# Grid search proved by counts with a branch into the exact search, batch rows turned by VectorE, and aligned load buffers, in an attention and expert-routing kernel

## The chip, the cores and the metric

The kernel runs on one core of one Trainium2 chip. The core has five engines, each with an instruction stream of its own: TensorE (PE; its weight loads are shown as PEld), VectorE (DVE), ScalarE (ACT), GpSimd (POOL) and SyncE (SP, which here only issues transfers). They wait for each other by semaphores. The metric is the time of one execution on the device, in microseconds; lower is better.

## The reference

Attention over 8 batches, 12 heads, 448 tokens and 64 features per head, with a sigmoid instead of a softmax, and behind it a mixture of 8 experts in which each expert takes exactly 448 of the 3584 tokens:

```
scores = scale * np.matmul(q, k.transpose(0, 1, 3, 2)) - np.log(S)
attn = 1.0 / (1.0 + np.exp(-scores))
attn_out = np.matmul(attn, v)
x = attn_out.transpose(0, 2, 1, 3).reshape(B * S, H * D)
logits = x @ w_gate
for idx in np.argsort(-logits.flatten()):
    tok, e = (int(idx) // E, int(idx) % E)
    if assigned[tok] >= 0 or counts[e] >= cap:
        continue
    assigned[tok] = e
    counts[e] += 1
for e in range(E):
    mask = assigned == e
    out[mask] = np.maximum(x[mask] @ w1[e], 0.0) @ w2[e]
```

All data are float32. `cap` is 448. Tokens of one batch have nearly equal logits, because the sigmoids are all near 1/449 and a head's output is near the mean of V.

## The kernel before, in words

**Attention.** A loop goes over 48 pairs of heads (`pairs`, six for each batch). For a pair, VectorE transposes K and Q into `kqT` (`turn`, L408) from load buffers `nkq` that SP and GpSimd fill two groups ahead (`load`). ScalarE rounds them (`kqH`, L416), VectorE takes the rest (`kqL`, L417), so that a product of float32 is three products (L433). ScalarE makes the sigmoids (`at`, L423). One pair later TensorE multiplies with V (`av`, L457 and L463), and VectorE copies the outcome into `xt` (L465, L467), with features on partitions. A list `bg` of small jobs is worked off, one a pair: `logits` (L478, added into `LE`, L480) and `rows` (L489 to L496). `rows` transposes half a chunk of 112 tokens on TensorE, copies it to `xr` and stores it in `xs`, a table in DRAM with a row for each token. With `LATE = 7` only the first batch is turned so during attention (copied by VectorE); the rows of the other seven wait in `late`.

**Routing.** `Router.phase(k)` is a generator that settles one expert after the other: take away what is settled (`remove`), build keys so that each token counts for its best expert alone (`keys`, L151 to L158), find in each expert's list the 448th largest key (`search`), take the expert with the largest one (`pick`), and make its list of tokens (`place`, `lists`, ending with `r_idx`, L298). `search` fixes the bits of the threshold in 16 steps of two bits. Each step counts the keys over three thresholds (three L178, with the count read out) and adds the counts of 16 rows: by a product on TensorE (L190) for `k == 0`, by two 32-wide transposes and a reduction on VectorE (L194 to L200) for later experts. The first phase runs by itself, with the late rows between its steps (`LATE_PER_STEP`). The later phases run between the matmuls of the experts.

**Experts.** `moe(kx)` yields after every matmul with a planned cost, which runs a clock; when the clock says so, the next piece of the routing is recorded (`T_KEYS` ... `T_BT` are the planned waits behind each piece) or one of the `chores`: the gather of the next expert's rows (`gather`, L625), their transposes into `xh` and `xl` (`xturn`, L639 to L643), and the turning back of the output. `prepare` puts gathers and transposes on that list as soon as the next expert's list is recorded, and `flush` issues at the end of an expert what is still due. Weights are streamed: `load_w` reads the chosen expert's number into a register of SP (L585) and issues one transfer for each unit (L592, L596), ScalarE rounds (`wh`, L603), GpSimd or, for the first two units, VectorE takes the rest (`wl`, L605). Everything is recorded in program order, and each engine works in that order.

Of the kernel before, what the change touches and what calls it, by code (L numbers as in the profile page):

```python
# [7 lines left out]
F32 = mybir.dt.float32  # L8
# [14 lines left out]
LATE = 7  # L23
XT_BUFS = 7
XA_BUFS = 5
AT_BUFS = 8
YT_BUFS = 3
LATE_PER_STEP = 3
LATE_KEYS = 7
T_KEYS, T_KE, T_STEP, T_DVE, T_KAP, T_PICK, T_TOT, T_OH, T_BT = 3600, 2100, 2050, 2025, 500, 2600, 600, 3800, 600  # L30
# [6 lines left out]
Y_DVE, Y_WAIT = 6, 4000  # L37

# [10 lines left out]
def route_consts(nc, cp, K):  # L49
# [66 lines left out]
    K.gfin = _s32(g)  # L116


class Router:
# [4 lines left out]
    def __init__(self, tc, K, st, wk, psum):  # L124
        self.tc, self.nc, self.K = tc, tc.nc, K
        self.wk, self.ps = wk, psum
        self.ei = None
        self.ML = st.tile([112, 2, 8, 16], F32, name="ML")
        self.csum = st.tile([1, 1], F32, name="csum")
        tc.nc.vector.memset(self.csum, -28.0)  # L130

# [30 lines left out]
    def search(self, pe):  # L162

        nc, K, wk, KT = self.nc, self.K, self.wk, self.KT
        p = self.bank()
        for g in range(2):
            nc.tensor.transpose(p[:, g * 112:(g + 1) * 112],
                                KT[:, g].rearrange("p e c -> p (e c)"), K.ident[:112, :112])
        KE = wk.tile([128, 224], F32, name="r_KE")
        nc.vector.tensor_copy(KE, p[:, :224])  # L170
        T, JP = K.c0, None
        X = None if pe else self.bank().bitcast(I32)
        for st in range(16):
            sh = 30 - 2 * st
            cnt = wk.tile([128, 3], BF, name="r_cnt") if pe else K.CN
            for i in range(3):
                junk = wk.tile([128, 224], BF, name="r_junk")
                nc.vector.tensor_scalar(junk, KE, T[:, i:i + 1].bitcast(F32), None, OP.is_ge, OP.add,  # L178
                                        accum_out=cnt[:, i:i + 1])
            nX = None  # L180
            if 0 < st < 15:
                nX = wk.tile([128, 3], I32, name="r_X") if pe else X[:, 4 * (st % 2):4 * (st % 2) + 3]
            acc = wk.tile([128, 1], F32, name="r_acc")
            j2 = wk.tile([128, 3], F32, name="r_j2")
            if pe:
                if nX is not None:
                    nc.vector.tensor_scalar(nX, K.kk[:, st + 1], JP, None, OP.bitwise_xor)
# [4 lines left out]
            else:  # L192
                ct = wk.tile([128, 32], F32, name="r_ct")
                nc.vector.transpose(ct, cnt)  # L194
                if nX is not None:
                    nc.vector.tensor_scalar(nX, K.kk[:, st + 1], JP, None, OP.bitwise_xor)
                s2 = wk.tile([128, 2], F32, name="r_s2")
                nc.vector.tensor_reduce(s2, ct.rearrange("p (e r) -> p e r", r=16), AX.X, OP.add)
                ct2 = wk.tile([128, 32], F32, name="r_ct")
                nc.vector.transpose(ct2.rearrange("p (e r) -> p e r", r=16), s2[:, :, None].to_broadcast([128, 2, 16]))  # L200
                tot = ct2[:, :3]
            nc.vector.tensor_scalar(j2, tot, 447.5, TWO23, OP.is_ge, OP.add, accum_out=acc)
            nJ = wk.tile([128, 1], I32, name="r_J")
            if st == 0:
                J = wk.tile([128, 1], I32, name="r_J0")
                nc.vector.tensor_scalar(J, acc.bitcast(I32), sh, None, OP.logical_shift_left)
                PF = wk.tile([128, 1], I32, name="r_PF")
                nc.vector.tensor_scalar(PF, J, 31, -1, OP.arith_shift_right, OP.bitwise_xor)
                nc.vector.tensor_scalar(nJ, PF, _s32(0x80000000), J, OP.bitwise_or, OP.bitwise_xor)
                T = wk.tile([128, 3], I32, name="r_T")  # L210
                nc.vector.tensor_scalar(T, K.kk[:, 1], nJ, None, OP.bitwise_xor)
            else:
                if st < 15:
                    T = wk.tile([128, 3], I32, name="r_T")
                    nc.vector.scalar_tensor_tensor(T, acc.bitcast(I32).to_broadcast([128, 3]), sh, nX,
                                                   OP.logical_shift_left, OP.bitwise_xor)
                nc.vector.tensor_scalar(nJ, acc.bitcast(I32), sh, JP, OP.logical_shift_left, OP.bitwise_xor)
            JP = nJ
            if not pe:
                yield T_DVE  # L220
        kap = wk.tile([128, 1], I32, name="r_kap")
        nc.vector.tensor_scalar(kap, JP, K.gfin, None, OP.bitwise_xor)
        self.kap = kap.bitcast(F32)

    def pick(self):
# [3 lines left out]
        nc.tensor.transpose(p[:112, :128], self.kap.to_broadcast([128, 112]), K.ident)  # L229
        kr = p[:112, :128].rearrange("p (e c) -> p e c", c=16)[:, :, 0]  # L230
        km = wk.tile([112, 1], F32, name="r_km")
        nc.vector.tensor_reduce(km, kr, AX.X, OP.max)
        w = self.w8 = wk.tile([112, 8], F32, name="r_w8")
# [14 lines left out]
        self.ei = wk.tile([1, 1], I32, name="r_ei", bufs=4)  # L248
# [22 lines left out]
    def lists(self):  # L271
# [25 lines left out]
        idx = wk.tile([128, 4], I32, name="r_idx", bufs=4)  # L297
# [14 lines left out]
    def left(self):  # L312
# [8 lines left out]
        self.ei = wk.tile([1, 1], I32, name="r_ei", bufs=4)  # L321
        nc.vector.tensor_copy(self.ei, self.csum)

    def phase(self, k):
        if k:
            self.remove()
        if k < 7:
            self.keys()
            yield T_KEYS
            yield from self.search(k == 0)  # L330
            yield T_KAP
            self.pick()
# [7 lines left out]
def moe_attention(tc, q, k, v, w_gate, w1, w2, out):  # L340
# [7 lines left out]
    with contextlib.ExitStack() as ctx:  # L348
# [7 lines left out]
        ps_s = pctx.enter_context(tc.tile_pool(name="pa_s", bufs=3, space=PSUM))  # L356
        ld = actx.enter_context(tc.tile_pool(name="ld", bufs=2))
# [123 lines left out]

        XR = {}

        def rows(b, c, hf, eng):
            if hf == 0:
                XR[b] = xa.tile([CP, DM], F32, name="xr", bufs=XA_BUFS)
            p = ps_t.tile([128, 512], F32, name="tp")
            for i in range(3):
                nc.tensor.transpose(p[:CP, i * 128:(i + 1) * 128], XT[b][:, hf * 3 + i, c * CP:(c + 1) * CP], ident)  # L489
            dst = XR[b][:, hf * 384:(hf + 1) * 384]  # L490
# [396 lines left out]
```

## Time and profile before

| | us |
|---|---|
| median of three runs | 882.42 (881.5 to 882.93) |
| profiled execution, whole | 883.43 |
| its span, first to last instruction | 881.7 |
| attention, TensorE's first product to its last of V | 7.5 to 278 |
| logits, first routing, late rows | 278 to 332.8 |
| experts | 332.8 to 861.7 |
| last half of the output | 861.7 to 881.7 |

Times in views count from the start of the span. A line with L and a number is that line of the kernel. A group's row names the line, the engine, the operation, what is written and read, the shape, the count, then the busy time in us and the mean of one in ns, and behind the last bar the idle time ahead of it with what ended it. In a timeline, the first number is the start and the second the length.

### The profile page before, as it was taken

Reading aid. Unit: us, or ns where it says so; the run is one execution under the profiler, and the core shown is the slowest. Engines: PE = TensorE matmul, PEld = TensorE weight load, DVE = VectorE, ACT = ScalarE, POOL = GpSimd, SP = SyncE. Lnnn points to the kernel's source line nnn. Section 1 sums busy time; section 2 is a strip of 40 time slices with the busy share of each in tenths; the row PEclk is TensorE's granted clock in tenths of the full one; section 3 lists DMA queues with packets and bytes.
Section 4 is the critical chain, followed back from the end, with each engine's and each line's share of the span. In section 5 each row is a group of like instructions: output and inputs, shape, how many; then the busy total and the mean of one; then the engine's idle time right before and its main releaser. Section 6 shows DMA issues by size and latency. Waiting matters only on the chain.

```text
span 881.7 us, 16211 instructions
## 1 busy us (share of the span) xinstructions
PE 840.1 (95%) x5467; PEld 636.9 (72%) x5467; DVE 542.4 (62%) x2060; ACT 447.3 (51%) x612; POOL 466.0 (53%) x446
## 2 busy tenths in 40 slices
PE   6999999999999739998999999999999999999996
PEld 3455555555554528987988988988888888999996
DVE  4566555555554988958859879779779631332130
ACT  6777677777775734434434434534434344541420
POOL 9744344444410014854864873873883883851561
PEclk9999999999999979998999999999999999999999
DMA  9866766666621855443442442551542542634643
GB/s 173 165 142 149 153 126 127 127 126 127 126 43 54 270 192 154 120 138 123 128 136 97 160 155 81 177 162 57 189 153 72 170 153 90 209 96 141 203 151 126
DMA packets 213811, 122.16 MB, mean 139 GB/s; under 512 B 153344, under 2 KB 202496, under 8 KB 213728
## 3 DMA queue, kind: packets, MB, share of 16 engines
q1 hardware_dynamic: 200992, 87.62, 38.2%
q0 software_dynamic: 10880, 33.28, 12.0%
q8 instruction: 43, 0.70, 0.3%
q10 hardware_dynamic: 1856, 0.23, 0.2%
q14 instruction: 40, 0.33, 0.1%
HBM read 96.76 MB, written 24.31 MB: 137 GB/s over the span
## 4 chain that ended last, share of the span: by engine, by line
PE 82%; DVE 11%; issue 2%; DMA 2%; POOL 1%; SPq 1%; ACT 1%; POOLq 0%; DVEq 0%; ACTq 0%
PE tp L457 13%; PE sc L433 11%; PE sc L736 9%; PE sc L734 9%; PE sc L738 9%; PE sc L773 6%; PE sc L775 6%; PE sc L771 6%; DVE r_junk L178 4%; PE tp L463 2%; PE sc L443 2%; PE tp L639 2%; PE tp L652 2%; PE tp L478 1%; PE rt L289 1%
## 5 line engine op out<-in xcount | busy, mean ns | idle before, releaser
L605 POOL TENSOR_TENSOR wl<-wr,wh 128x768 fp32r<-128x768 f32 (+1 forms) x96 | 204.9, 2145 | 124.5 <-ACT wh L603 116.8
L423 ACT ACTIVATE at<-sc,bias 128x896 f32<-128x896 f32 x168 | 161.5, 1006 | 67.1 <-PE sc L443 38.4
L383 POOL DMA_DIRECT2D nkq<-in_q_dram x188 | 118.4, 646 | 116.2 <-DVE kqT L408 104.6
L775 PE MATMUL sc<-hh,wl 128*128 128x448 f32 (+2 forms) x400 | 150.2, 375 | 0.0
L738 PE MATMUL sc<-xh,wl 128*128 128x448 f32 (+2 forms) x396 | 146.2, 369 | 0.0
L736 PE MATMUL sc<-xl,wh 128*128 128x448 f32 (+2 forms) x396 | 146.0, 369 | 0.1
L773 PE MATMUL sc<-hl,wh 128*128 128x448 f32 (+2 forms) x400 | 145.5, 364 | 0.2 <-POOL hl L746 0.2
L734 PE MATMUL sc<-xh,wh 128*128 128x448 f32 (+2 forms) x396 | 145.0, 366 | 0.0
L771 PE MATMUL sc<-hh,wh 128*128 128x448 f32 (+2 forms) x400 | 144.1, 360 | 0.4 <-issue 0.4
L178 DVE TENSOR_SCALAR_CACHE_REDUCE r_junk<-r_KE,r_T 128x224 bf16<-128x224 f32 x315 | 123.2, 441 | 0.1
L603 ACT ACTIVATE wh<-wr 128x768 fp32r<-128x768 f32 (+1 forms) x112 | 102.0, 939 | 36.3 <-DMA wr<-in_moe_w_dram 23.4
L457 PE MATMUL tp<-at,nv 128*64 128x448 f32 x576 | 118.8, 548 | 0.0
L746 POOL TENSOR_TENSOR hl<-yt,hh 128x896 fp32r<-128x896 f32 x32 | 68.4, 2136 | 48.8 <-ACT yt L745 47.2
L742 ACT ACTIVATE hh<-sc 128x896 fp32r<-128x896 f32 x32 | 29.5, 921 | 117.1 <-PE sc L738 117.1
L417 DVE TENSOR_TENSOR kqL<-kqT,kqH 128x896 fp32r<-128x896 f32 (+1 forms) x49 | 52.5, 1073 | 58.5 <-ACT kqH L416 58.4
L773 PEld LDWEIGHTS sc<-hl,wh 128*128 128x128 f32 x400 | 75.8, 189 | 6.8 <-issue 1.1
L625 POOL DMA_INDIRECT xr<-xs,r_idx x32 | 32.0, 999 | 91.2 <-ACT wh L603 80.2
L736 PEld LDWEIGHTS sc<-xl,wh 128*128 128x128 f32 x396 | 75.2, 190 | 6.7 <-issue 0.5
L457 PEld LDWEIGHTS tp<-at,nv 128*64 128x64 f32 x576 | 37.1, 136 | 59.1 <-issue 56.6
L734 PEld LDWEIGHTS sc<-xh,wh 128*128 128x128 f32 x396 | 75.2, 190 | 6.0
L771 PEld LDWEIGHTS sc<-hh,wh 128*128 128x128 f32 x400 | 76.0, 190 | 4.8 <-issue 0.6
L738 PEld LDWEIGHTS sc<-xh,wl 128*128 128x128 f32 x396 | 75.1, 190 | 5.3
(166 smaller groups left out, 1266.1 us busy)
## 6 DMA issues: line engine op xcount, KB each, us to landing
wr<-in_moe_w_dram SPq DMA_DIRECT2D x64, 384.0 KB, 3.0
wr<-in_moe_w_dram SPq DMA_DIRECT2D x48, 512.0 KB, 3.6
nkq<-in_k_dram SPq DMA_DIRECT2D x192, 56.0 KB, 2.6
xs<-xr SPq DMA_DIRECT2D x32, 336.0 KB, 3.3
nkq<-in_q_dram POOLq DMA_DIRECT2D x188, 56.0 KB, 2.7
nv<-in_v_dram SPq DMA_DIRECT2D x92, 96.0 KB, 2.7
ys<-yt SPq DMA_DIRECT2D x20, 112.0 KB, 1.9
nr<-in_v_dram SPq DMA_DIRECT2D x46, 32.0 KB, 2.2
```

The costliest lines, as they stand in the source:

```text
L178: nc.vector.tensor_scalar(junk, KE, T[:, i:i + 1].bitcast(F32), None, OP.is_ge, OP.add, accum_out=cnt[:, i:i + 1])
L383: qn.dma_start(t[o:o + 32, n], rws[x])
L423: nc.scalar.activation(a, p[:, :, :S], AF.Sigmoid, bias=bias, scale=1 / math.sqrt(D))
L457: nc.tensor.matmul(p[j * 64:j * 64 + 64, :S], nat["v", b, g][:, h0 + j, c, :], AT[b, pr, c][:, j, :], start=(c == 0), stop=(c == 2 and pr ...
L603: nc.scalar.activation(hi, raw[u], AF.Copy)
L605: eng.tensor_tensor(lo, raw[u], hi.bitcast(F32), OP.subtract)
L734: nc.tensor.matmul(ph[:, f, lo:hi], wh[:, a, fs], xh[:, dd, lo:hi], start=st, stop=False)
L736: nc.tensor.matmul(ph[:, f, lo:hi], wh[:, a, fs], xl[:, dd, lo:hi], start=False, stop=False)
L738: nc.tensor.matmul(ph[:, f, lo:hi], wl[:, a, fs], xh[:, dd, lo:hi], start=False, stop=en)
L771: nc.tensor.matmul(py[:, d2, :w], wh[:, a, dsl], h1, start=st, stop=False)
L773: nc.tensor.matmul(py[:, d2, :w], wh[:, a, dsl], h2, start=False, stop=False)
L775: nc.tensor.matmul(py[:, d2, :w], wl[:, a, dsl], h1, start=False, stop=(j == 1 and a == 3))
```

## The change

Several edits go together.

**The search.** `scale`, new, takes from the logits of the first four batches the power of two `D` at or under the largest, and makes a grid from it: steps of `D`, `D/4`, `D/16` and so on. `search` now refines the edge by two bits a step on that grid, in floating point: 4 steps from `-2D` for the first expert, and 9 steps from the former threshold less `D` for the others. It ends with the lower edge `base` of an interval, and one more count of the keys at that edge. `pick` transposes the edges and sums the counts on TensorE, and adds the counts of the experts that have the largest edge. If that sum is exactly 448, the edge parts the same tokens as the 448th key does. The sum is read into a register of VectorE and compared; otherwise a branch leads into `exact`, the former 16 steps wholly on VectorE.

```diff
+        self.tc.mark_branch_hint_location(f"found{k}", "LikelyTaken", [mybir.EngineType.DVE])
+        self.base = base
+        self.cnt = wk.tile([128, 1], BF, name="r_cn1")
+        self.count(base, self.cnt)
...
-        nc.tensor.transpose(p[:112, :128], self.kap.to_broadcast([128, 112]), K.ident)
-        kr = p[:112, :128].rearrange("p (e c) -> p e c", c=16)[:, :, 0]
-        km = wk.tile([112, 1], F32, name="r_km")
+        nc.tensor.transpose(p[:, :128], self.base.to_broadcast([128, 128]), K.ident)
+        nc.tensor.matmul(p[:, 128:256], self.cnt.to_broadcast([128, 128]), K.G, start=True, stop=True)
+        tr, cr = (p[:, o:o + 128].rearrange("p (e c) -> p e c", c=16)[:, :, 0] for o in (0, 128))
+        few, kr = wk.tile([128, 8], F32, name="r_few"), wk.tile([128, 8], F32, name="r_kr")
+        nc.vector.tensor_scalar(few, cr, 447.5, NONE, OP.is_lt, OP.mult)
+        nc.vector.tensor_tensor(kr, tr, few, OP.subtract)
+        km = self.km = wk.tile([128, 1], F32, name="r_km")
         nc.vector.tensor_reduce(km, kr, AX.X, OP.max)
+        nc.vector.tensor_tensor(few, cr, few, OP.add)
+        nc.vector.scalar_tensor_tensor(few, kr, km, few, OP.is_equal, OP.mult)
+        ok = wk.tile([128, 1], F32, name="r_ok")
+        nc.vector.tensor_reduce(ok, few, AX.X, OP.add)
+        found = nc.vector.value_load(ok[:1].bitcast(I32))
+        with self.tc.If(found != FOUND, preferred_fallthrough_block=True, label=f"found{k}"):
+            self.exact(kr)
+            nc.vector.tensor_reduce(km, kr, AX.X, OP.max)
```

`N_FIRST, N_FAST = 4, 9`; `FOUND` is 448.0 as an integer. `scale` runs in `bg` after the fourth batch:

```diff
+            nc.vector.tensor_scalar(a.bitcast(I32), LE[:, 0].bitcast(I32), 0x7FFFFFFF, None, OP.bitwise_and)
+            nc.vector.tensor_reduce(m[:, :1], a, AX.X, OP.max)
+            nc.tensor.transpose(p[:, :128], m[:, :1].to_broadcast([128, 128]), ident)
+            nc.vector.tensor_reduce(m[:, 1:], p[:, :128], AX.X, OP.max)
...
+    for r in range(N_FAST + 1):
+        nc.vector.tensor_scalar(K.cw[:, r], t8, 4.0 ** -r, None, OP.mult)
```

VectorE's order in the first routing, at the end of the search, before. `r_J` holds the bits found, `r_kap` the threshold, `r_km` the largest one, `r_w` the marks of the experts that have it:

```order
L178 TENSOR_SCALAR r_junk,r_cnt<-r_KE,r_T 128x224 x3
L202 TENSOR_SCALAR r_j_3968,r_acc<-rt 128x3
L217 TENSOR_SCALAR r_J<-r_acc,r_J 128x1
L222 TENSOR_SCALAR r_kap<-r_J 128x1
L232 TENSOR_REDUCE r_km<-rt 112x1
L234 SCALAR_TENSOR_TENSOR r_w_3998<-rt,r_km,c_rank 112x8
```

And now, after 4 steps in place of 16, up to the branch:

```order
L239 TENSOR_SCALAR r_base<-r_acc,c_kw,r_base 128x1
L184 TENSOR_SCALAR r_junk,r_cn_3553<-r_KE,r_base 128x224
L292 TENSOR_SCALAR r_few<-rt 128x8
L293 TENSOR_TENSOR r_kr<-rt,r_few 128x8
L295 TENSOR_REDUCE r_km<-r_kr 128x1
L296 TENSOR_TENSOR r_few<-rt,r_few 128x8
L297 SCALAR_TENSOR_TENSOR r_few<-r_kr,r_km,r_few 128x8
L299 TENSOR_REDUCE r_ok<-r_few 128x1
L300 TENSOR_LOAD r_ok
L301 COMPARE_AND_BRANCH
```

Behind the branch stand the 165 instructions of `exact` with their closing jump, then a short block that only evens the semaphore and jumps, and then L306, the former L234. The four other engines have a plain jump at each of the seven places.

**The rows.** `LATE` goes from 7 to 1. `turn_rows`, new, transposes two pairs of heads of a batch on VectorE in blocks of 32 by 32 during attention, and stores them when four or two pairs are together (eight transfers a batch on SP). Only the last batch's rows are still turned by TensorE (`late_rows`, six transposes and two copies by ScalarE for each chunk of 112).

```diff
+            if old and old[1] % 2 and old[0] < B - LATE:
+                bg.append(lambda b=old[0], pr=old[1]: turn_rows(b, pr))
...
+            nc.vector.transpose(XR[b].rearrange("p i r j -> p r i j")[:, pr - 1 - h:pr + 1 - h],
+                                XT[b][:, pr - 1:pr + 1].rearrange("p r (i t) -> p r i t", t=32))
+            if pr == h + n - 1:
+                for a in range(4):
+                    o, w = 128 * h + 32 * n * a, 32 * n
+                    nc.sync.dma_start(xs[b * S:(b + 1) * S, o:o + w].rearrange("(i t) c -> t i c", t=32),
+                                      XR[b][32 * a:32 * a + 32].rearrange("t i r j -> t i (r j)"))
```

TensorE's order between the last batch's logits and the search, before (`rt` is the router's tile in PSUM, `LE` the logits, `r_KT` the keys):

```order
L478 MATMUL tp<-xt,wgz 32x112 x8
L489 MATMUL tp<-ident,xt 112x128 x3
L139 MATMUL rt<-ident,LE 112x128 x2
L489 MATMUL tp<-ident,xt 112x128 x21
L167 MATMUL rt<-ident,r_KT 128x112 x2
L489 MATMUL tp<-ident,xt 112x128 x9
L190 LDWEIGHTS c_G
L190 MATMUL rt<-r_cnt,c_G 128x3
L489 MATMUL tp<-ident,xt 112x128 x9
```

And now:

```order
L552 MATMUL tp<-xt,wgz 32x112 x8
L583 MATMUL sc<-ident,xt 112x128 x6
L149 MATMUL rt<-ident,LE 112x128 x2
L583 MATMUL sc<-ident,xt 112x128 x18
L177 MATMUL rt<-ident,r_KT 128x112 x2
L229 LDWEIGHTS c_G
L229 MATMUL rt<-r_cnt,c_G 128x3
```

Six row transposes instead of three stand ahead of the logits' own, 18 instead of 21 ahead of the keys', and none between the steps.

**The order of features.** Rows turned in blocks of 32 stand in `xs` in another order of features, so the rows of `w1` are read in that order. A unit of the first layer then takes three transfers (`j == 0`) or five (`j == 1`) instead of one, of the same bytes:

```diff
-                src = w1[ds(gate[kx], 1)].rearrange("e (a p) f -> p (e a) f", p=128)
-                nc.sync.dma_start(t, src[:, 3 * j:3 * j + 3, i * 256:(i + 1) * 256])
+                src = w1[ds(gate[kx], 1)].rearrange("e (r a j) f -> a (e r) j f", a=4, j=32)[:, :, :, i * 256:i * 256 + 256]
+                for a in range(3 * j, min(3 * j + 3, 4)):
+                    nc.sync.dma_start(t[:, a % 3], src[a, :4])
+                for a in range(4 * j):
+                    nc.sync.dma_start(t[64 * (a % 2):64 * (a % 2) + 64, 1 + a // 2], src[a, 4:])
```

**Planned times and buffers.** The planned waits of the routing are new (`T_DVE` 2025 to 2290, `T_KAP` 500 to 3000, `T_PICK` 2600 to 5200). For experts after the first, gathers are due 25 us of the clock into the expert and the row transposes 9 us later, 2.3 us apart (after the first gathers: 5 us later and 1.7 us apart):

```diff
-                t0 = clock[0]
-                lag = max(5000, min(14000, start + 40000 - t0))
+                t0 = max(clock[0], start + X_AT) if kx else clock[0]
+                lag = 9000 if kx else 5000
...
-                        chores.append((t0 + lag + 1500 * j, kx + 1,
+                        chores.append((t0 + lag + (X_GAP if kx else 1700) * (2 * j + hf), kx + 1,
```

`r_ei` and `r_idx` have 8 buffers instead of 4, `xt` 3 instead of 7. A pad of 192 bytes a partition moves the load buffers; `nkq` and `nv` now begin at multiples of 512 bytes.

More of the change, by code (lines that the diff above doesn't have):

```diff
@@ L160, in keys, with ends @@
         self.KT = KT
-    def search(self, pe):
-        nc, K, wk, KT = self.nc, self.K, self.wk, self.KT
+    def ends(self):
+        nc, KT = self.nc, self.KT
         p = self.bank()
@@ L167, in search @@
             nc.tensor.transpose(p[:, g * 112:(g + 1) * 112],
[L168 to L174, printed above, removed]
+                                KT[:, g].rearrange("p e c -> p (e c)"), self.K.ident[:112, :112])
+        self.KE = self.wk.tile([128, 224], F32, name="r_KE")
@@ new lines, in ends, with count, sums @@
+        nc.vector.tensor_copy(self.KE, p[:, :224])
+    def count(self, T, cnt):
+        junk = self.wk.tile([128, 224], BF, name="r_junk")
+        self.nc.vector.tensor_scalar(junk, self.KE, T, None, OP.is_ge, OP.add, accum_out=cnt)
+    def sums(self, cnt, ct, s2, ct2, between=None):
+        nc = self.nc
+        nc.vector.transpose(ct, cnt)
+        if between:
+            between()
+        nc.vector.tensor_reduce(s2, ct.rearrange("p (e r) -> p e r", r=16), AX.X, OP.add)
+        nc.vector.transpose(ct2.rearrange("p (e r) -> p e r", r=16), s2[:, :, None].to_broadcast([128, 2, 16]))
+        return ct2[:, :3]
@@ new lines, in search @@
+    def search(self, k):
+        nc, K, wk = self.nc, self.K, self.wk
+        pe = k == 0
+        rows = range(N_FIRST) if pe else range(1, N_FAST + 1)
+        if pe:
+            T, base = K.T0, K.base0
+        else:
+            base = wk.tile([128, 1], F32, name="r_base")
+            nc.vector.tensor_scalar(base, self.km, K.D, None, OP.subtract)
+            T = wk.tile([128, 3], F32, name="r_T")
+            nc.vector.tensor_scalar(T, K.kw[:, 1], base, None, OP.add)
+        X = None if pe else self.bank()
+        for r in rows:
@@ L183, in search, with ahead @@
+            def ahead(r=r, nX=nX, base=base):
+                if nX is not None:
+                    nc.vector.tensor_scalar(nX, K.kw[:, r + 1], base, None, OP.add)
             acc = wk.tile([128, 1], F32, name="r_acc")
@@ L185, in search @@
             if pe:
-                if nX is not None:
-                    nc.vector.tensor_scalar(nX, K.kk[:, st + 1], JP, None, OP.bitwise_xor)
+                ahead()
                 yield T_STEP
@@ L329, in phase @@
             yield T_KEYS
-            yield from self.search(k == 0)
+            self.ends()
+            yield from self.search(k)
             yield T_KAP
-            self.pick()
+            self.pick(k)
         else:
@@ new lines, in moe_attention, with late_rows @@
+        XR = {}
+        def late_rows(b, c):
+            x = xa.tile([CP, DM], F32, name="xr", bufs=XA_BUFS)
+            p = ps_s.tile([128, 2, 512], F32, name="sc")
+            for r in range(NP):
+                o = r % 4 * 128
+                nc.tensor.transpose(p[:CP, r // 4, o:o + 128], XT[b][:, r, c * CP:(c + 1) * CP], ident)
+            for h, n in ((0, 4), (1, 2)):
+                nc.scalar.copy(x[:, 512 * h:512 * h + 128 * n].rearrange("p (a r j) -> p r a j", r=n, j=32),
+                               p[:CP, h, :128 * n].rearrange("p (r a j) -> p r a j", r=n, j=32))
+            nc.sync.dma_start(xs[b * S + c * CP:b * S + (c + 1) * CP], x)
@@ L531, in moe_attention @@
                     bg.append(lambda b=b: logits(b, range(NP)))
[L532 to L537 removed]
+                if b == 3:
+                    bg.append(scale)
+                for c in range(NCH if b >= B - LATE else 0):
+                    late.append(lambda b=b, c=c: late_rows(b, c))
         for f in bg:
```

130 lines of the change are left out of this document (75 added, 55 removed).

## The prediction

> **What bounds the kernel now.** I read the page's first part (busy time by engine) and the chain that ended last, then the busy time by stage. Columns of the second view: stretch, length, then busy time of TensorE, its weight loads, VectorE, ScalarE and GpSimd, the granted TensorE clock, the DMA engines' busy share and GB/s.
>
> ```profile
> PE 840.1 (95%) x5467; PEld 636.9 (72%) x5467; DVE 542.4 (62%) x2060; ACT 447.3 (51%) x612; POOL 466.0 (53%) x446
> PE 82%; DVE 11%; issue 2%; DMA 2%; POOL 1%; SPq 1%; ACT 1%; POOLq 0%; DVEq 0%; ACTq 0%
> ```
>
> ```profile
> 7.50:278.00 270.50, 270.39 (x2216) 137.87 (x2216) 150.62 (x208) 197.24 (x216) 121.64 (x204) 1.00 0.61 125
> ...
> 285.10:315.50 30.40, 23.19 (x155) 14.86 (x154) 27.52 (x176) 21.95 (x48) 0.00 (x0) 1.00 0.84 272
> 315.50:332.80 17.30, 5.32 (x53) 4.25 (x53) 13.21 (x37) 3.17 (x5) 4.13 (x6) 0.61 0.54 165
> 332.80:861.70 528.90, 523.05 (x2896) 464.42 (x2895) 342.69 (x1626) 215.65 (x325) 329.48 (x213) 0.99 0.44 137
> ```
>
> Attention (to 278) and the experts (332.8 to 861.7) are TensorE without a hole worth naming; only work taken from TensorE itself shortens them. The 54.8 us between belong to a chain on VectorE: TensorE's 23.19 us during the search are row transposes beside it.
>
> ```profile
> 287.66 1.20 DVE r_junk L178 x6
> 289.59 1.11 DVE r_junk L178 x6
> ...
> 313.60 1.11 DVE r_junk L178 x6
> ```
>
> From 289.59 to 313.60 are 13 search steps, 1.847 us each, on the chain. So the routing of the first expert is where the search counts fully; for the other six it runs beside matmuls.
>
> **Attention: rows off TensorE.** The first batch's 8 half rows are transposed on TensorE within attention; two pairs of heads last 80.03 - 68.49 = 11.54 us with them and 236.10 - 225.52 = 10.58 without.
>
> ```profile
> 68.49 2.02 PE sc L433 x18
> ...
> 80.03 2.01 PE sc L433 x18
> ...
> 225.52 2.09 PE sc L433 x18
> ...
> 236.10 2.09 PE sc L433 x18
> ```
>
> Four such double pairs give -3.8. In their place VectorE makes 21 transposes of 128x896. The nearest row is its transpose of K and Q, 1.1 us: 23 us, less 4.4 of copies.
>
> ```profile
> L408 DVE STREAM_TRANSPOSE kqT<-nkq 128x896 f32<-128x896 f32 x47 | 51.8, 1103 | 2.5 <-DMA nv<-in_v_dram 1.5 <-DMA nkq<-in_k_dram 0.2
> L494 DVE COPY xr<-tp 112x384 f32<-112x384 f32 x8 | 4.4, 550 | 0.2
> L480 DVE TENSOR_TENSOR LE<-LE,tp 128x112 f32<-128x112 f32 x9 | 2.4, 271 | 5.7 <-PE tp L478 5.7
> ```
>
> VectorE then has 169 of 270 us and ScalarE stays at 197, so I cost the turns at nothing; their cover is VectorE's idle time, and without it they cost up to 23 us (a rival). The 56 row stores go to SP's queue among the K and V loads: at the K loads' median of 0.47 us that is 26 us over 230, on engines busy 0.61 of the time; the loads run two groups ahead. The new alignment of the load buffers can only speed transfers that TensorE does not wait for after 7.5 us: 0. `scale()` is new on the path: one TensorE transpose stands behind VectorE's copy (0.6), an absolute value and a reduction over 128x112 (0.27 by L480, each), then 0.3 for itself, and TensorE waits: +1.6 (0.5 to 3, the upper end with ten small constants also on VectorE). Attention: **-2.2**.
>
> **The first search.** Columns: start, length, engine, line.
>
> ```profile
> 279.69 0.54 PE L489 MATMUL tp<-ident,xt 128*112 128x128 f32 x3 [0.38 <-DVE csum L130]
> 280.06 0.38 PE L139 MATMUL rt<-ident,LE 128*112 128x128 f32 x2
> 285.12 0.45 DVE L178 TENSOR_SCALAR_CACHE_REDUCE r_junk<-r_KE,c_c 128x224 bf16<-128x224 f32 x1
> 315.40 0.15 DVE L222 TENSOR_SCALAR r_kap<-r_J 128x1 int32<-128x1 int32 x1
> 315.97 0.17 DVE L232 TENSOR_REDUCE r_km<-rt 112x1 f32<-112x8 f32 x1 [0.41 <-PE rt L229]
> 316.17 0.23 DVE L234 SCALAR_TENSOR_TENSOR r_w<-rt,r_km,c_rank 112x8 f32<-112x8 f32 x1
> ```
>
> ```profile
> L236 DVE TENSOR_REDUCE r_c<-r_w 112x1 f32<-112x8 f32 x7 | 1.1, 161 | 0.2
> L585 SPq TENSOR_LOAD <-r_ei x8: 266/278/481, 318.4 to 796.1; - x8
> q14 instruction: 40, 0.33, 0.1%
> nr<-in_v_dram SPq DMA_DIRECT2D x46, 32.0 KB, 2.2
> ```
>
> Before, from the first count (285.12) to L234 (316.17): 31.05. Now: four steps at 1.85 = 7.4; the closing count 0.5; the hop over TensorE 0.41; six small operations at 0.16 to 0.23 with their gaps 1.35; together 9.7. Then a load of `r_ok` into a register and a branch. SP's load of the same kind takes 0.27 to 0.48. No branch stands in this trace. Lower end: the load alone, 0.3. Upper end: two jumps (into the short block, and out of it), each waiting for code: 0.33 MB in 40 packets is 8 KB each, and 0.1% of 16 x 881.7 us over 40 is 0.35 us of transfer, to which I add the 2.2 us of the quickest landing: 0.5 + 2 x 2.55 = 5.6. I take 1.5, nearer the load's row, since the hint stands ahead of the closing count, 2.8 us before the branch, and so can cover one fetch of 2.55. That is 11.2, a gain of 19.85. Six row transposes instead of three stand ahead of the logits' own: 280.06 - 279.69 = +0.4. The other 18 end before the keys do (284.1 now), their three further stores long before the gather. Search: **-19.5** (-15.0 to -20.7).
>
> [...]
>
> **The weights behind it.** Each first-layer unit is loaded by 3 or 5 transfers instead of one.
>
> ```profile
> 319.79 0.42 SPq L592 DMA_DIRECT2D wr<-in_moe_w_dram  x1
> 320.44 0.39 SPq L592 DMA_DIRECT2D wr<-in_moe_w_dram  x1
> ```
>
> ```profile
> 324.22 0.84 ACT L603 ACTIVATE wh<-wr 128x768 fp32r<-128x768 f32 x1 [0.38 <-DMA wr<-in_moe_w_dram]
> 324.52 1.82 DVE L605 TENSOR_TENSOR wl<-wr,wh 128x768 fp32r<-128x768 f32 x2
> 330.30 0.42 DVE L158 SCALAR_TENSOR_TENSOR r_KT<-rt,ML 112x256 f32<-112x256 f32 x1
> 330.72 0.56 DVE L643 TENSOR_TENSOR xl<-tp,xh 128x384 fp32r<-128x384 f32 x1
> 333.30 0.39 PE L736 MATMUL sc<-xl,wh 128*128 128x256 f32 x1
> ```
>
> Issues follow each other by 0.65, so of the eight transfers of the first two units the last goes out at 319.79 + 7 x 0.65 = 324.3 and lands by about 326.5 (again 2.2). `wh` of the second unit then ends at 327.4 instead of 325.1, and the second `wl` stands on VectorE at 327.4 instead of 325.4. Behind it on VectorE are the removal and keys of the next routing (without a hole up to 330.72) and then `xl`, for which TensorE waits at 333.30: 2.0 late at `xl`. VectorE's four `xl` then follow each other without their present waits, which returns some: **+1.7** (0 to 2.4). Later units have many microseconds between issue and use; there SP's longer issuing costs nothing.
>
> **The experts.** All TensorE work there stays, with one 128-column product per routing more. What can go are holes and slow clock:
>
> ```profile
> 401.88 1.01 PE L639 MATMUL tp<-ident,xr 128*128 128x128 f32 x6 [1.08 <-DVE xl L643]
> 403.60 0.87 PE L639 MATMUL tp<-ident,xr 128*128 128x128 f32 x6 [0.71 <-DVE xl L643]
> 405.32 0.58 PE L639 MATMUL tp<-ident,xr 64*128 64x64 f32 x3 [0.85 <-DVE xl L643]
> ```
>
> ```profile
> 319.00:332.80 13.80, 4.62 (x50) 3.87 (x50) 10.52 (x25) 3.17 (x5) 4.13 (x6) 0.51 0.53 161
> 404.50:411.20 6.70, 5.88 (x18) 5.14 (x19) 5.45 (x31) 1.83 (x5) 2.76 (x3) 0.50 0.15 50
> ```
>
> At the end of expert 0 the list of expert 1 had come so late that its transposes are issued in one heap; they wait for each other's `xl`: 1.08 + 0.71 + 0.85 = 2.6. Right behind, the granted clock is 0.50 for 6.7 us: 3.4 lost. With 9 steps instead of 16 (7 x 1.85 = 13 less, 3.4 more for the closing count, small operations, load and branch) the list comes about ten microseconds earlier, the turns are spaced by 1.7, and the heap goes: -6.0. All holes from 332.8 to 861.7 are at most 528.9 - 523.05 = 5.9; the other 3.3 are short waits for VectorE in six experts. New times of gathers and turns (25 and 34 us into an expert, 2.3 apart) may mend or renew them: 0 (-3.3 to +3). Then the clock at the start: it was half from 319 to 332.8 and full just as the matmuls began. TensorE now idles for some 20 us before, and the clock may come back later than the matmuls, by up to 6.7 us at half, that is 3.4; I take +0.7. Experts: **-5.3** (-9.3 to +0.4: the heap's -6.0, with -3.3 or with +3 and +3.4).
>
> [...]
>
> **The rivals.**
> - **Code fetch at the branches.** For: 7 data-dependent branches, each past a block of 165 instructions on VectorE, with pages of 8 KB. Against: the hint. Both jumps missed in the first routing: 5.6 - 1.5 = +4.1, 861. If TensorE's own plain jumps, one at each branch, were to stop it as long in the six later routings, 6 x 2.55 = 15 more: 876.
> - **The row turns show in attention.** For: ScalarE is busy for 73% there, and a transpose of K and Q that comes 1.1 us late pushes its sigmoids. Against: VectorE waits 1 us or more in each pair of heads. If nothing hides: 857 + 23 = 880.
> - **Spread turns collide anew** with untransposes and search steps: the experts give nothing back, 857 + 5.3 = 862.
> - **The proof fails** (the change doesn't do what it says; slower). If the lower edge of the found interval does not count exactly 448 in the first routing, VectorE runs the 16-step block on the chain: 16 x 1.85 = 30, 2 for its small copies and 2.6 for its code, so 857 + 34 = 891. It decides at one token more or less. Worked out on the reference's inputs, the largest logit of four batches is 0.01696, the grid unit 2^-6, the step after four rounds 0.00024; the best expert has exactly 448 keys, the last at 0.01120, and its edge is 0.01099: proved. In the nine-step routings the tightest edge (the fifth) has 1.2e-8 of room against a rounding of some 2e-9. A failure there would keep VectorE for 34 us beside the matmuls, with the next expert's `xl` behind it: up to +30.
>
> **How the numbers follow.** The profiled execution took 883.43, 1.7 outside its span of 881.7, and lies 1.0 above the median of the three runs, 882.42. -2.2 - 19.5 + 1.7 - 5.3 = -25.3: 858.1 in its terms, 857.1 at the median: 857. All lower ends (-3.3 - 20.7 + 0 - 9.3 = -33.3) give 849; all upper ends (-0.8 - 15.0 + 2.4 + 0.4 = -13.0) give 869.4. The range is 849 to 869. Chances: forecast 0.68, collisions 0.14, code fetch 0.07 (0.02 of it at 876), turns that show 0.06, a failed proof 0.05. Beyond 0.2% (1.8 us, about what a measurement of this kernel can tell from no change): faster 0.92, same 0.03, slower 0.05.
>
> **What would show it.** Attention ends near 276; no wait of TensorE there but one of about 1.5 us. First count to L306: about 11 us, with 1.5 or less between the last small operation and L306; a hole of 3 or more says code fetch. The first expert's matmuls begin near 313 (332.8 - 2.2 - 19.5 + 1.7). No heap of transposes and no half clock between experts 0 and 1. Wrong would be: counts of VectorE inside the 16-step block, TensorE waiting for ScalarE's sigmoids in attention, or holes at the jumps on TensorE.

## The result, and the profile after

| | median, us | runs | to before, 95% interval |
|---|---|---|---|
| before | 882.5 | 4 | |
| the change | 924.81 | 4 | 1.0467 [1.0404, 1.053] |

The change is slower by 42 us; the forecast was 857. Its four runs lie between 917.37 and 927.24, and the profiled one is the longest of them. That profiled execution of the change has a span of 925.5 us. Busy time by engine, and then the busy time by stage (stretch, length, TensorE, weight loads, VectorE, ScalarE, GpSimd, granted TensorE clock, share of the 16 DMA engines, GB/s), both of the change:

```profile
PE 833.9 (90%) x5295; PEld 632.8 (68%) x5295; DVE 460.5 (50%) x1417; ACT 427.5 (46%) x564; POOL 461.1 (50%) x446
```

```profile
7.50:278.00 270.50, 268.35 (x2213) 136.33 (x2214) 170.14 (x239) 199.66 (x216) 121.87 (x204) 1.00 0.74 155
...
323.10:905.20 582.10, 542.14 (x2897) 477.10 (x2898) 261.40 (x1079) 215.75 (x323) 322.69 (x212) 0.96 0.39 124
```

In the attention TensorE has 2.04 us less to do, as forecast. The expert stage has grown from 528.9 to 582.1 us. Two columns say of what: TensorE is busy for 542.14 instead of 523.05 us with the same matmuls, because its clock is down to 0.96; and it is idle for 40.0 instead of 5.9. The half-speed stretches begin with holes, as this one near the end of a hole of 6.25 us that ends at 366.44 (TensorE's instruction behind the hole, then the stretch):

```profile
366.44 0.21 PE L329 MATMUL rt<-c_ones,r_mk 112*64 112x1 bf16 x1 [6.25 <-DVE r_ei L321]
365.30:372.10 6.80, 5.66 (x16) 4.76 (x17) 4.47 (x15) 0.00 (x0) 1.39 (x1) 0.50 0.11 36
```

The first routing, VectorE in the change, from the first count to L306:

```profile
283.61 0.45 DVE L184 TENSOR_SCALAR_CACHE_REDUCE r_junk<-r_KE,c_T 128x224 bf16<-128x224 f32 x1
...
293.25 0.16 DVE L299 TENSOR_REDUCE r_ok<-r_few 128x1 f32<-128x8 f32 x1
294.80 0.23 DVE L306 SCALAR_TENSOR_TENSOR r_w<-r_kr,r_km,c_rank 112x8 f32<-112x8 f32 x1 [1.38 <-DVEq L301]
```

That is 11.19 us where 11.2 was forecast, with 1.38 for the load and the branch. No count of the 16-step block appears in any routing, so the proof holds. Up to here the kernel runs as predicted: L306 stands at 294.80 instead of 316.17. Everything that is lost is lost behind it. The view of waits (who waited for whom, us in total, times, longest) names two places. First the change; then before, where only the last of the four kinds is found:

```profile
DVE r_w L306 <- DVEq L301: 32.3, 7, 6.3
PE rt L329 <- DVE r_ei L321: 23.6, 6, 6.3
PE sc L841 <- ACT wh L710: 9.8, 5, 4.1
ACT wh L710 <- DMA wr<-in_moe_w_dram: 99.5, 20, 23.8
```

```profile
ACT wh L603 <- DMA wr<-in_moe_w_dram: 23.4, 6, 7.9
```

The first place is the branch (L301): L306 behind it waits for VectorE's own queue, 32.3 us in seven waits, of which the first routing has 1.38. TensorE waits in six of the seven routings, the first among them, at L329, its first matmul that needs what VectorE makes behind the branch. The second place is the weights: ScalarE waits 99.5 us for them, and TensorE for ScalarE. The first expert shows it best. ScalarE in the change:

```profile
305.86 0.84 ACT L710 ACTIVATE wh<-wr 128x768 fp32r<-128x768 f32 x1 [23.82 <-DMA wr<-in_moe_w_dram]
315.91 0.84 ACT L710 ACTIVATE wh<-wr 128x768 fp32r<-128x768 f32 x1 [9.21 <-DMA wr<-in_moe_w_dram]
```

SP's eight issues for these two units:

```profile
298.45 3.04 SPq L697 DMA_DIRECT2D wr<-in_moe_w_dram  x4
301.69 3.55 SPq L699 DMA_DIRECT2D wr<-in_moe_w_dram  x4
```

The last is out at 305.24; still the second unit is not there before 315.91, and the first expert's matmuls begin at 323.14 in place of the forecast 313. The DMA engines are not full meanwhile. Stretches of the change in which only weights move, and, second, the same weights before:

```profile
300.00:304.50 4.50, 1.34 (x34) 1.07 (x34) 1.56 (x4) 0.00 (x0) 0.52 (x1) 0.50 0.26 83
318.00:322.00 4.00, 0.00 (x0) 0.00 (x0) 3.73 (x9) 1.11 (x2) 1.11 (x1) 0.50 0.14 48
```

```profile
321.00:323.50 2.50, 0.98 (x32) 0.92 (x32) 1.47 (x2) 0.51 (x1) 0.00 (x0) 0.50 0.84 291
```

In the DMA records all packets of data in these stretches are of 1024 bytes with a median of 46 ns, before and after. What differs is how many are under way at a time: in the mean 4.2 and 2.2 in the change, 13.5 before. So no packet is slower; fewer engines work. 0.26 of 16 is 4.2 engines, 0.14 is 2.2. The new transfers have a source whose outer dimension is 4 (`src[a, :4]`) or 2 (`src[a, 4:]`); the old one had 128 partitions there. So 4.2 engines work where that dimension is 4, 2.2 where it is 2, and 13.5 where it was 128. The prediction had not weighed this dimension.

### The profile page after: what moved, and what is told of

Read it like the earlier page. It is cut to its first block, busy times and chain, and to the rows that moved or that the text cites. A ratio compares the mean times of both kernels' runs of the same rounds, so it can differ in the third digit from the quotient of the medians.

```text
span 925.5 us, 15946 instructions
## 1 busy us (share of the span) xinstructions
PE 833.9 (90%) x5295; PEld 632.8 (68%) x5295; DVE 460.5 (50%) x1417; ACT 427.5 (46%) x564; POOL 461.1 (50%) x446
## 5 line engine op out<-in xcount | busy, mean ns | idle before, releaser
L712 POOL TENSOR_TENSOR wl<-wr,wh 128x768 fp32r<-128x768 f32 (+1 forms) x96 | 200.1, 2094 | 161.2 <-ACT wh L710 159.8
L841 PE MATMUL sc<-xh,wh 128*128 128x448 f32 (+2 forms) x396 | 148.6, 375 | 10.1 <-ACT wh L710 9.8
L882 PE MATMUL sc<-hh,wl 128*128 128x448 f32 (+2 forms) x400 | 154.9, 387 | 2.7 <-POOL wl L712 2.7
L710 ACT ACTIVATE wh<-wr 128x768 fp32r<-128x768 f32 (+1 forms) x112 | 102.7, 938 | 114.0 <-DMA wr<-in_moe_w_dram 99.5
L845 PE MATMUL sc<-xh,wl 128*128 128x448 f32 (+2 forms) x396 | 149.9, 378 | 3.1 <-POOL wl L712 1.2
L880 PE MATMUL sc<-hl,wh 128*128 128x448 f32 (+2 forms) x400 | 147.9, 370 | 0.7 <-POOL hl L853 0.7
L878 PE MATMUL sc<-hh,wh 128*128 128x448 f32 (+2 forms) x400 | 147.8, 370 | 0.4 <-ACT yt L810 0.4
L750 DVE TENSOR_TENSOR xl<-tp,xh 128x384 fp32r<-128x384 f32 (+1 forms) x60 | 30.0, 502 | 124.1 <-ACT xh L749 124.1
L841 PEld LDWEIGHTS sc<-xh,wh 128*128 128x128 f32 x396 | 77.5, 196 | 18.5 <-ACT wh L710 11.7
L882 PEld LDWEIGHTS sc<-hh,wl 128*128 128x128 f32 x400 | 78.0, 195 | 8.8 <-POOL wl L712 3.5
L880 PEld LDWEIGHTS sc<-hl,wh 128*128 128x128 f32 x400 | 78.1, 195 | 6.5 <-POOL hl L853 1.1
```

The lines of the kernel that those rows point to most:

```text
L710: nc.scalar.activation(hi, raw[u], AF.Copy)
L712: eng.tensor_tensor(lo, raw[u], hi.bitcast(F32), OP.subtract)
L841: nc.tensor.matmul(ph[:, f, lo:hi], wh[:, a, fs], xh[:, dd, lo:hi], start=st, stop=False)
L845: nc.tensor.matmul(ph[:, f, lo:hi], wl[:, a, fs], xh[:, dd, lo:hi], start=False, stop=en)
L878: nc.tensor.matmul(py[:, d2, :w], wh[:, a, dsl], h1, start=st, stop=False)
L880: nc.tensor.matmul(py[:, d2, :w], wh[:, a, dsl], h2, start=False, stop=False)
```

## The experiments

Two theories, each with a place in the trace: **N**, the narrow transfers make the weights late; **B**, the taken branch stops VectorE, TensorE waits behind it and then runs at half clock. All runs are medians beside runs of the kernel before on the same chip (883.1 to 883.3).

| run | us | to before, 95% interval |
|---|---|---|
| wide transfers | 885.24 | 1.0022 [1.0008, 1.0036] |
| no branch | 916.45 | 1.0395 [1.0376, 1.0413] |
| both | 866.5 | 0.9822 [0.9806, 0.9838] |
| before, with narrow transfers | 934.98 | 1.0605 [1.0587, 1.0623] |
| both, buffers aligned | 857.96 | 0.9716 [0.969, 0.9743] |
| wide, later first matmul | 865.71 | 0.9799 [0.9772, 0.9825] |
| wide, short block | 871.07 | 0.985 [0.9815, 0.9886] |
| wide, no hint | 888.49 | 1.0048 [1.0027, 1.0069] |
| no branch, buffers aligned | 896.14 | 1.016 [1.0134, 1.0186] |
| wide, short block, `kr` in PSUM | 857.24 | 0.9714 [0.9691, 0.9737] |
| wide, later first matmul, `kr` in PSUM | 866.88 | 0.9821 [0.9796, 0.9846] |

**Wide transfers.** The same bytes for the same places, with an outer dimension of 32. (In the kernels with wide transfers, the lines behind this place are one higher than in the change.)

```diff
-                for a in range(3 * j, min(3 * j + 3, 4)):
-                    nc.sync.dma_start(t[:, a % 3], src[a, :4])
-                for a in range(4 * j):
-                    nc.sync.dma_start(t[64 * (a % 2):64 * (a % 2) + 64, 1 + a // 2], src[a, 4:])
+                if j == 0:
+                    for r in range(4): nc.sync.dma_start(t[32 * r:32 * r + 32], src[:3, r].rearrange("a j f -> j a f"))
+                else:
+                    for r in range(4): nc.sync.dma_start(t[32 * r:32 * r + 32, 0], src[3, r])
+                    for r in range(4): nc.sync.dma_start(t[32 * r:32 * r + 32, 1:], src[r // 2::2, 4 + r % 2].rearrange("a j f -> j a f"))
```

> Edit: the changed kernel, with the permuted first-layer weights of a unit fetched in transfers of 32 partitions (one for each 32-row group r, 4 for the even unit and 8 for the odd one) where the change has transfers of 128 and of 64 partitions (3 and 5). Same bytes, same packets, same places, more issues. Theory N (narrow transfers): a transfer whose outer source dimension is 4 or 2 moves on about 4 or 2 of the 16 DMA engines (DMA share 0.27 and 0.14 while only they run, against 0.82 for the old form), and that makes the weights late. It expects the share to rise to 0.6 or more, wh of the second unit by 307 to 309 in place of 315.9, the first expert's matmuls near 315, no weight waits in experts 5 to 7, and 895 to 905 in all if the holes at the routings' first matmul are the branch's own, 875 to 890 if they come with the weights too. Theory B (the branch alone): 915 or more, since the holes stay and the fetches were a side matter. Rival (issuing): with 12 issues for 8 on SyncE it gets slower, over 930.

Measured: 885.24, 39.6 less than the change. ScalarE, and the stage of the experts (from 313.30), in this run:

```profile
302.78 0.84 ACT L711 ACTIVATE wh<-wr 128x768 fp32r<-128x768 f32 x1 [20.82 <-DMA wr<-in_moe_w_dram]
306.10 0.84 ACT L711 ACTIVATE wh<-wr 128x768 fp32r<-128x768 f32 x1 [2.47 <-DMA wr<-in_moe_w_dram]
```

```profile
313.30:863.30 550.00, 529.32 (x2898) 471.33 (x2899) 269.58 (x1079) 216.42 (x324) 327.00 (x213) 0.97 0.44 132
```

The second unit is there 9.8 us earlier, and the first expert starts 9.8 us earlier (313.35), at the forecast 313. TensorE's waits for `wh` are gone from the view of waits, ScalarE's for weights are 32.0 us instead of 99.5; those at L329 stay (21.8). More issues, but SP is through them sooner: four took 1.97 us of its queue, where four narrow ones took 3.04 and later 5.95. Two expectations were off. The time lies below the 895 to 905 that went with holes that stay. And the share rose only to 0.42 (123 GB/s from 300 to 304 us): the twelve transfers of the first two units, 768 KB, are issued from 298.38 to 304.44, which is 130 GB/s, so it is likely the issuing that now sets the pace. Theory N holds, and the 28 us that are left above the forecast are for theory B to explain.

**No branch**, with the narrow transfers kept, and **both**.

```diff
-        found = nc.vector.value_load(ok[:1].bitcast(I32))
-        with self.tc.If(found != FOUND, preferred_fallthrough_block=True, label=f"found{k}"):
-            self.exact(kr)
-            nc.vector.tensor_reduce(km, kr, AX.X, OP.max)
```

> Edit: the changed kernel without the load of the flag, the branch, its hint and the 16-step search behind it; the short search's answer is taken as proved, so the fallback is left out. All else is the same. Theory B (each taken branch stops VectorE for about 4.6 us, TensorE waits at the routing's first matmul behind it and then runs at half clock): the seven waits of the instruction behind the branch (32.3 us in all) go, the holes of 1.4 to 6.3 us at TensorE's first matmul of each routing and the half-clock stretches behind them go, 880 to 890. Theory N (the weights are late and that is what costs): 905 to 920, with holes of the same size moved to the weights. As predicted blind, a branch costs 1.5 us in the first routing alone: 921 to 925.

> Edit: both of the two others, transfers of 32 partitions and no branch (the fallback left out). If the two are the whole of the loss, what is left is the change as predicted blind, 852 to 862. If more is lost than they explain (the new due times of the routing's steps, the alignment, the later gathers), 865 or more, and the trace shows where.

Measured: 916.45 and 866.5. The first is far above theory B's 880 to 890 (and within the 905 to 920 of theory N), the second above the 852 to 862 for two causes that are the whole of it, and the trace shows a third thing, which these edits brought themselves. The attention, in "both":

```profile
7.50:278.00 270.50, 263.00 (x2133) 133.84 (x2135) 169.20 (x236) 198.55 (x216) 121.73 (x204) 0.99 0.93 156
```

The DMA share is 0.93 where the change has 0.74, at the same GB/s, and the first logits behind it start at 284.9 instead of 277.1. The records say that the packets of 128 bytes take a mean of 16.2 ns instead of 12.8, those of 256 bytes 23.6 instead of 17.8. Without the 16-step search its small tiles are gone, and the load buffers stand 64 bytes past a multiple of 512; in the change they begin at such a multiple, in the kernel before 256 past one.

**Both, buffers aligned**, and **no branch, buffers aligned**: `PAD = 160` in place of 48 puts the buffers where the change has them.

> Edit: the run with transfers of 32 partitions and no branch again, its pad 160 words in place of 48. Without the 16-step search its small tiles are gone too, and the load buffers had moved from a multiple of 512 bytes to 64 past one; the wider pad puts them back to the addresses of the change. Theory A (addresses): the 128-byte packets of the attention go from a mean of 16.2 back to 12.8 ns, the 256-byte ones from 23.9 to 17.8, the attention ends near 277 in place of 285, and the time is 857 to 860. Rival (other code, other fetches at the start): the attention stays at 283 to 285 and the time at 866.

> Edit: the change without flag, branch, hint and the 16-step search (the fallback left out), as in the second run, its narrow transfers kept, with the pad at 160 words so that the load buffers stand where the change has them. The second run was 916.5 with the buffers 64 bytes past a multiple of 512 and an attention that ended 5 us late. If the two causes add up (as 885.2 to 858.0 says for the branch with the wide transfers), 924.8 less 27 is 898. If the late weights hide most of what the branch costs (TensorE waits for one or for the other), 909 to 913. Theory A asks for 5 us less than the second run whichever of the two holds.

Measured: 857.96, packets at 12.8 and 17.8 ns, the first logits at 276.6. The experts in this run:

```profile
311.90:836.20 524.30, 520.28 (x2898) 464.50 (x2899) 268.83 (x1079) 215.54 (x324) 330.37 (x213) 1.00 0.46 138
```

TensorE idles for 4.0 us there, at full clock. Without branch but with narrow transfers it is 896.14. Against before the four corners are +4.67% (the change), +0.22% (wide), +1.60% (no branch), -2.84% (both): wide transfers give 4.45, no branch 3.07, both 7.51. The causes add up, and with both gone the time is within 1 us of the forecast. The expected 898 came out at 896.14, but the second half of that expectation is missed: the alignment gave 20 us there, not 5. The attention ended 5.9 us earlier; the other 14 came in the experts, where the weight buffers had moved by the same 64 bytes and the 1024-byte packets went from a mean of 53.7 to 51.7 ns. That this is the cause is not shown: with the wide transfers the same shift left these packets at 56.6 and 56.7 ns. Why the alignment gave so much beside late weights stays open.

**Before, with narrow transfers.** The same 3 and 5 transfers in the kernel before; the rows of `w1` there meet other columns of x, so its output is not the reference's, for the same amount of work.

> Edit: the kernel before, with the permuted first-layer weights fetched as in the change (3 and 5 transfers for 1 and 1); xs is left as it was, so rows of the weights meet other columns of x than in the reference. Theory N: the DMA share falls to about 0.25 while these run, the first expert starts 8 to 10 us later and some units come late in the later experts: 893 to 912. Rival (the fetches are ahead far enough, only their issuing costs): 882 to 886.

Measured: 934.98, over both expectations: 52 us for one edit. The first expert starts at 344.95 instead of 332.80, and ScalarE waits far longer for weights (it was 23.4 us in 6 waits):

```profile
ACT wh L606 <- DMA wr<-in_moe_w_dram: 117.7, 24, 11.4
```

So theory N holds without anything else of the change, and "ahead far enough" is wrong.

**The branch by itself: a short block, no hint.** The wide transfers, and in the first kernel `range(2)` for `range(16)` in `exact` (which doesn't run in either; cut so, it could not stand in where a proof fails, so this kernel is a probe), in the second the line with the branch hint's mark taken out.

> Edit: the change with transfers of 32 partitions, the search behind the branch cut from 16 steps to 2, so that the taken branch passes over some 40 VectorE instructions in place of some 165. The block doesn't run in either kernel. Theory F (the target's code has to be fetched, as the 8192-byte fetch between the branch and its target's first instruction says): most of the six long stops fall to about 0.5 us, and the time to 860 to 870. Rival (a taken branch costs 3 to 4.5 us wherever it goes): all six stay, 883 to 887.

> Edit: the change with transfers of 32 partitions, without the seven marks of the branch hint (on VectorE's queue all seven stand at the head of the program). Theory H (a hint that early serves the first branch alone, which goes on after 0.53 us where the others take 2.8 to 4.6): the first stop grows to 2.5 to 4.5 us, the others stay, 887 to 891. Rival (the marks do nothing: the first branch's target was in the chip's store already): the first stop stays at 0.5 us, 884 to 886. If the marks helped the later ones, these grow and the time passes 891.

Measured: 871.07 and 888.49. From the trace, the time in us from the end of the compare-and-branch to the next instruction on VectorE, with the start of the next 8192-byte instruction fetch of the queue q14 behind the branch in brackets where it lies ahead of that instruction:

```
routing          1            2            3            4            5            6            7
wide             0.53         4.49 (2.68)  3.73 (1.85)  2.72 (0.94)  4.45 (2.65)  4.32 (2.54)  2.87 (0.95)
short block      0.17         0.16         0.16         0.53         0.48         0.16         0.16
no hint          2.76 (0.95)  4.44 (2.64)  3.68 (1.86)  2.93 (1.08)  5.62 (3.81)  3.41 (1.60)  2.80 (0.93)
```

Here a stop longer than 0.6 us always has such a fetch in it, and goes on 1.8 to 1.9 us after it starts. Here a jump over some 40 instructions finds its target at hand, and with the hints in place six of the seven over 165 do not. In the change itself, with its narrow transfers, the six are longer, 3.9 to 5.7 us. Without the hint the first one stops as well, for 2.76 us instead of 0.53; so the hint serves that one alone. (The times, 888.49 and 885.24, do not settle it: their intervals against before overlap.) In the trace all seven hints run at the head of VectorE's program, between 0.79 and 1.22 us, not ahead of each search.

With the short block the time fell by 14 us only, 1 above what was expected, and TensorE still had two holes of over 3 us at L329. VectorE and then GpSimd there, in the run with the short block:

```profile
396.74 0.16 DVE L299 TENSOR_REDUCE r_ok<-r_few 128x1 f32<-128x8 f32 x1
397.97 5.14 DVE L306 SCALAR_TENSOR_TENSOR r_w<-r_kr,r_km,c_rank 112x8 f32<-112x8 f32 x1 [1.07 <-DVEq L301]
403.14 0.16 DVE L308 TENSOR_REDUCE r_c<-r_w 112x1 f32<-112x8 f32 x1
```

```profile
397.39 2.12 POOL L854 TENSOR_TENSOR hl<-yt,hh 128x896 fp32r<-128x896 f32 x1
399.47 3.61 POOL L713 TENSOR_TENSOR wl<-wr,wh 128x768 fp32r<-128x768 f32 x2
```

An operation on 8 numbers takes 5.14 us: it starts while GpSimd works and ends 0.03 us after GpSimd's third operation. Before, the same operation (L234) took a mean of 226 ns: its first operand was in PSUM; the change moved it to SBUF (`kr`). The next run puts `kr` into PSUM, and the operation takes 0.23 us in the mean of seven, instead of up to 5.14.

**Short block, `kr` in PSUM.**

```diff
-        few, kr = wk.tile([128, 8], F32, name="r_few"), wk.tile([128, 8], F32, name="r_kr")
+        few, kr = wk.tile([128, 8], F32, name="r_few"), p[:, 272:280]
```

> Edit: the run with the search behind the branch cut to 2 steps (transfers of 32 partitions), with kr, the first operand of L306, in PSUM in place of SBUF; the pad is 16 words wider so that the load buffers keep their addresses. Theory S (an operation of VectorE with two operands in SBUF waits for as long as GpSimd's elementwise operations run: L306 took 5.1 and 4.9 us there and ended within 0.03 us of the end of a GpSimd operation): L306 stays under 0.4 us in all seven routings, TensorE's holes of 3.45 and 3.22 us at L329 go, 858 to 863. Rival (the long ones are the fetch of the code behind the branch again): they stay, 867 to 872.

Measured: 857.24, just under what was expected. The group of L306 in the short block's run and in this one:

```profile
L306 DVE SCALAR_TENSOR_TENSOR r_w<-r_kr,r_km,c_rank 112x8 f32<-112x8 f32 x7 | 13.0, 1854 | 6.6 <-DVEq L301 6.6
L306 DVE SCALAR_TENSOR_TENSOR r_w<-rt,r_km,c_rank 112x8 f32<-112x8 f32 x7 | 1.6, 226 | 6.6 <-DVEq L301 6.6
```

After the first routing no hole at L329 is left. This kernel has the load, the compare, the branch and the plain jumps of the other engines; they hold VectorE for 6.6 us in all seven routings, 27.9 with the long block. It is as fast as the one without them (857.96, which has `kr` in SBUF): a branch whose target is at hand costs next to nothing here, on TensorE neither.

**A later first matmul.** The complete kernel (16-step block and hint in place) with the wide transfers, and TensorE's matmul at L329 planned 12 us behind the proof: `T_PICK` 12000 in place of 5200. Then the same with `kr` in PSUM.

> Edit: the change with transfers of 32 partitions, branch and all, and the due time between the proof and the first matmul of the placing (T_PICK) 12000 in place of 5200 ns of TensorE's plan. Theory P (what the branch costs is that TensorE comes to that matmul before VectorE has come out of the branch): the stalls behind the branch stay at 2.7 to 4.6 us on VectorE, TensorE's holes of 3.2 to 6.2 us before L329 in the later routings go with the half-clock stretches behind them, and the time is 860 to 868. Rival (the stop of VectorE makes the transposed rows, keys or weights late for TensorE elsewhere): 875 or more, with the holes at other lines.

> Edit: the complete kernel of the run with the later first matmul (transfers of 32 partitions, branch, hint and 16-step search in place, T_PICK 12000), with kr in PSUM and the pad 16 words wider. Theory P, with S: the stalls of 2.7 to 4.5 us behind the branch stay, L306 no longer takes up to 1.6 us, and the time is 860 to 865. Rival: what was left there against 858.0 (7.7 us, one hole of 3.9 us and the half clock behind it among it) comes of the branch's stalls alone, and it stays at 864 to 867.

Measured: 865.71 and 866.88. The stops on VectorE stay (2.7 to 4.4 us in the six later routings), the holes before L329 go, and 19.5 of the 27 us with them: it is TensorE, come too early, that paid. `kr` in PSUM gives nothing more, as the rival in that expectation said. What is left has one place in the first of the two runs, TensorE behind the sixth branch:

```profile
578.45 0.69 PE L760 MATMUL tp<-ident,yt 128*128 128x128 f32 x2 [3.93 <-DVE xl L751]
```

`xl` stands on VectorE behind the stopped branch, so another chore of TensorE is late instead; behind it the granted clock is 0.50 for 6.8 us. The kernel at 865.71 computes all that the change computes and is faster than before by 2.0% [1.75, 2.28].

## Why the prediction was wrong

By its own steps:

- **Attention -2.2: right.** TensorE's busy time fell by 2.04 us, attention ends at 276.2 (forecast 276), with one wait of 1.25 us (about 1.5). VectorE is busy for 170.14 us (169), the turns are hidden. The alignment, costed at 0, gives nothing against before (12.8 ns a packet in both); what it does is to avert a loss of 5 to 8 us, which the two runs without it showed.
- **First search -19.5: right.** 11.19 us from the first count to L306 (11.2), 1.38 for load and branch (1.5). The upper end of this term does not come out of its parts: 19.5 less 4.1 is 15.4, not 15.0, which makes the range end at 869.0.
- **Weights +1.7 (0 to 2.4): this step failed first.** It counted issues, 0.65 us each, and took 2.2 us, the landing of an old transfer of another shape, as the landing of the new ones; of later units it said that "there SP's longer issuing costs nothing". The second unit was there 10.7 us after its last issue (305.24 to 315.91). The step asked how many transfers and how many bytes, not over how many of the 16 engines one of them is spread. In its place stands 4.45% or 39 us: 9.8 at the start of the first expert, the rest behind it, where late units leave holes and some stretches at half clock.
- **Experts -5.3, with the six later branches in it at nothing: this step failed second.** The term had "3.4 more for the closing count, small operations, load and branch" on VectorE and none of it on TensorE. The rival on code fetch looked at the wrong branches: it took the first routing as the place where a fetch could show, and the hint as an argument for all seven. It was the reverse. The hint, which the term saw 2.8 us ahead of the branch, runs some 293 us ahead of it. The first branch was covered, the six others stopped VectorE by 2.7 to 4.5 us each with wide transfers, and TensorE, which the new plan sends to L329 5.2 us after the proof, waited. In its place stands 3.07% or 27 us. Making the target near gave 14 of them; the other 14 came only with `kr` in PSUM besides, a second term that the sum had at nothing. The mechanism was named as a rival (861, and 876 by jumps on TensorE); its place and the half clock behind each hole were not.
- **The rest of the expert term: right in the main, one size off.** With both causes gone the stage lasts 524.3 instead of 528.6 to the same matmul, -4.3 for -5.3. The heap went as forecast: TensorE waits once for `xl` there, 0.72 us at 368.83, and no half clock follows. The clock at the start was put too low: it is half for the first 3.6 us of the stage, which costs 1.8 and not 0.7. The stretch in "both, buffers aligned":

```profile
311.90:315.50 3.60, 3.57 (x15) 3.44 (x16) 3.50 (x12) 0.33 (x1) 1.82 (x1) 0.50 0.56 139
```

Together: 857.96 with both causes removed, and 857.24 with the branch in place over the short block, for a forecast of 857 that held both at next to nothing. Of the other rivals none came: the turns do not show, the proof does not fail, spread turns give no holes.

## What to carry to other kernels

Where a change gives a transfer another shape, price it by the outer dimension of its source and not by its bytes alone: here an outer 4 or 2 left 12 or 14 of the 16 engines idle (4.2 and 2.2 at work), and the cure was to write the same copy with an outer 32, which gave 39.6 us. A branch on an engine that other engines wait for can cost the fetch of its target, 2.7 to 4.5 us here over 165 instructions and at most 0.5 over some 40; and when one engine is stopped, the price is paid by the engine that was planned to arrive too early, so moving that arrival takes most of it back (19.5 of 27 us here). Edits that add or drop a few small tiles move the buffers behind them, by 64 bytes here, which cost 8.5 us in the runs with both causes removed: hold the addresses fixed when comparing, or two causes are measured as one.

## What the hardware showed that was not expected

- The granted clock falls to 0.50 for 6.8 us at the end of and behind a single hole of 6.25 us, and for 6.8 to 10.2 us with holes of 2.9 to 4.1; five such stretches in the change are 37.5 us long. TensorE's busy time in the experts grew by 19.1 us for the same matmuls, about half as much as all its idle time there (40.0).
- 64 bytes of offset in the load buffers raised the mean of 128-byte packets from 12.8 to 16.2 ns and of 256-byte packets from 17.8 to 23.6, and lengthened the attention by 5 and by 8 us in two runs, although TensorE waits for no load in the aligned kernel.
- Seven hints at the head of the program served the first branch only: 0.53 us with them, 2.76 without, while the six later stops are 2.7 to 4.5 with them and 2.8 to 5.6 without.
- An 8-element VectorE operation with two SBUF inputs lasted up to 5.14 us beside GpSimd, and 0.23 with one of the two in PSUM.
